# Fused attention and Mish MLP on one core: a planned issue order replaced by a fixed list, with paired last query steps

## Chip, core and metric

One core of one Trainium2 chip. The metric is device time in microseconds (us) of one execution. Engines: PE is TensorE, DVE is VectorE, ACT is ScalarE, POOL is GpSimd, SP is SyncE, which here only issues DMAs.

## What is computed

```python
q_rot, k_rot = rotate(q), rotate(k)          # 4 batches, 8 heads, 576 positions, 64 wide
attn = softmax(q_rot @ k_rot.T / 8)
x = (attn @ v).transpose(0, 2, 1, 3).reshape(2304, 512)
h = x @ w_in                                 # 512 x 2048
g = h * tanh(softplus(h))                    # Mish
out = g @ w_out                              # 2048 x 512
```

## The kernel before

**Work.** Heads go in pairs, P = 0 to 15, four pairs to a batch. A pair's 576 queries are five steps: t = 0 to 3 of 128 queries, t = 4 of 64. A step (`step`, L744; `exact_step`, L725, for batch 0) has PE make the scores of both heads (`scores`, L626), DVE the row maxima (L656), ACT the exponentials with their row sums (L658), and DVE the sum plus 1e-9 and the reciprocal (L667, L669), one head at a time. At t = 4 the two heads of a pair share one score tile: 64 rows each, written by 64x64 matmuls for P < 8 (float32), and by a block-diagonal copy of the queries, `xd`, for P >= 8 (three terms, L642).

From batch 1 on, the weights of the softmax are split into two float16 parts (`weights_hi` on POOL or ACT, `weights_lo` on DVE, L679) in the tile `ew`, and a transposing DMA turns them. At t = 4, DVE first copies the second head's 64 rows to the upper partitions (L766). Batch 0 is turned by PE instead (`turned`, L683), with copies out of PSUM on ACT or DVE. `av` (L772) multiplies by V and leaves x as two float16 parts, for queries 0 to 255 (half 0) and 256 to 575 (half 1).

**The MLP** runs per batch and half, c = 0 to 7. `h_unit` makes 16 first products of 12 matmuls (L1014), ACT the Mish (L1019), `h_split` two float16 parts g (L1029, L1033). `p_sub` makes 16 second products of 12 matmuls (L1050); after every fourth ACT scales the result out (L1058) and issues the store.

**Weights.** Both arrive as 64-bit floats, 2 MB for each of four quarters of `w_in` and of `w_out`. A quarter is staged in a `Home` (tiles that are idle at that time: g, parts of w2, xt, stg, qk), its maximum is taken (L870), and it is decoded in four blocks by `decode` (L900): ACT scales the high words (L908); POOL, ACT or DVE shifts the low words (L910 to L913); DVE merges twice (L914, L917); ACT or DVE makes the first float16 part (L924); POOL or DVE the second (L928). That is 32 blocks in all. A quarter's load waits until the tiles of its home are read out.

**Order.** The program first lists all operations with their dependencies and the engines they may run on (`Plan.op`, L183). Then `Plan.order` (L220) plays a model of the engines, with priorities shifted by the table `ORDER` (L70), and fixes each engine's sequence. While its model has PE idle before 130 us, it puts matmuls on the identity matrix (fills, L1166) ahead of the next PE operation. FRONT, SLOTS and the W1/W2 lists (L31 to L51) set where steps, loads and decoding enter the list.

Of the kernel before, what the change touches and what calls it, by code (L numbers as in the profile page):

```python
# [30 lines left out]
W1L = [0, 0, 0, 2]  # L31
W1S = [3, 5, 3, 4]
W1D = [4, 10, 6, 9]
VA = 4
W2L = [3, 4, 6, 4]
W2D = [9, 13, 10, 13]
PRE0 = 15
WSH = 2
FRONT = 13
TR = 107 / 128  # L40
ALPHA = 7.992
SLOTS = [
    [1, 2, 4, 7, 12, 13, 13, 15, 16, 17, 17, 20, 21, 26, 26, 28, 29, 31],
    [10, 10, 12, 13, 14, 17, 18, 22, 23, 25, 28, 29, 31],
# [8 lines left out]
LATE = 24  # L53
PREP = [7, 5, 0, 13]
PSH = [25, 1, 822]
# [3 lines left out]
WARM = 130000  # L59
SKEEP = 1  # L60
QH = [[0], [0], [0, 1], [1], [0, 1]]
CUT = 320
SWITCH = 1400
DWELL = 920.788
PEN = 800
PENP = 183.99
HOLD = 0
PE, ACT, DVE, POOL, SP = "PE", "ACT", "DVE", "POOL", "SP"
ROPED = (0,)
ORDER = {}  # L70
for _row in """
    load_ident: =-891.8
    load_cs: 0=-4725.3 1=-2736.9
    prep_k: 0=-1685.8 1=1345.9 2=-3283.2 3=-1440.2 4=-2527.3 5=1365.9 6=-3350.9 7=-727.6 8=7228.2 9=1123 10=4507.3
        11=2436.8 12=1246.7 13=1266.3 14=531.9 15=-496
    prep_q: 0=-830.4 1=-2158.7 2=191.3 3=-532.3 4=894.2 5=1315.9 6=3277.5 7=923.3 8=5272.9 9=1626 10=4380.1 11=390.1
        12=5017.8 13=-412.3 14=-701.7 15=568.3
    load_v: 0=3994.1 1=5478 2=4090 3=4703.6 4=1637.8 5=6310.7 6=1937 7=2445.7 8=6111.3 9=6287.7 10=6432.3 11=6598.3
        12=1354.1 13=3922.6 14=5016.1 15=521.1
    w1_load: 0=3231.7 1=2580 2=2629.3 3=2601.7  # L80
    step: 0_0=-5011.8 0_1=-3915.2 1_0=-899.4 1_1=-3704.2 2_0=-768.3 2_1=-4320.3 3_0=-57 3_1=-170.5 0_2=1152
        0_3=-3148.4 0_4=-1518.5 1_2=2864.7 1_3=517.3 1_4=1108.3 2_2=776.3 2_3=-820.2 2_4=-3724.7 3_2=2490.2
        3_3=-1004.1 3_4=2186.6 4_0=-10265.9 4_1=-6834.6 4_2=-9928.1 4_3=-8511 4_4=-8735.2 5_0=-5295.7 5_1=-2535.4
        5_2=909.3 5_3=-4406.8 5_4=-1375 6_0=-4151.1 6_1=-1144.1 6_2=-446.8 6_3=-2426.2 6_4=-479.5 7_0=-5518.7
        7_1=-1224.1 7_2=-2119.2 7_3=-6982.4 7_4=-2612.3 8_0=-3202.1 8_1=-1414 8_2=204.1 8_3=2292.3 8_4=1625.1
        9_0=-5959.7 9_1=-4121.4 9_2=-6528.3 9_3=-2553.3 9_4=-6549.4 10_0=619.3 10_1=4327.5 10_2=-1607.1 10_3=641
        10_4=3369 11_0=1381.8 11_1=4866.8 11_2=1584.4 11_3=4685.9 11_4=4821.5 12_0=183.8 12_1=130.2 12_2=440
        12_3=981.1 12_4=-4305.9 13_0=-2179.5 13_1=-1019.4 13_2=-2104.5 13_3=1203.6 13_4=1964.2 14_0=255.3 14_1=-3296.6
        14_2=-1022.2 14_3=-3430.1 14_4=-4749.2 15_0=7309.3 15_1=12247.6 15_2=9741.9 15_3=12817.5 15_4=7465.4
    w1_scale: 0=-4916.9 2=-4591.2 3=-7163 1=-6494.3  # L90
    w2_load: 0=3752.3 1=6199.2 3=1533.5 2=4425.7
    v_amax: 0=-205.1 1=770.6 2=6910.8 3=384.2
    w1_decode: 0=-373 2=274.9 3=-427.1 1=494.1
    undo_h: 0_0=2142.2 0_2=2646.4 0_3=-6332.5 0_1=-910 1_0=-17085.8 1_1=-10926.9 1_2=-11192.1 1_3=-10149.8
# [24 lines left out]
        1_0_0=7256.9 1_0_1=724.9 1_0_2=2708.6 1_0_3=5613.4 1_1_0=5578.5 1_1_1=-240.8 1_1_2=2524.8 1_1_3=4870.4
        1_2_0=-2595.2 1_2_1=2569.1 1_2_2=1251.7 1_2_3=2314.6 1_3_0=8909.1 1_3_1=2527.9 1_3_2=6624.3 1_3_3=8988.5  # L120
        2_0_0=5216.6 2_0_1=4475.8 2_0_2=6685.1 2_0_3=5076.5 2_1_0=2015.2 2_1_1=3967.5 2_1_2=2759.6 2_1_3=-1754.1
        2_2_0=-543.3 2_2_1=-3395.8 2_2_2=-202.5 2_2_3=-415.9 2_3_0=7117.2 2_3_1=7249.2 2_3_2=10558.9 2_3_3=6213.1
        3_0_0=10859.4 3_0_1=5235.1 3_0_2=12710 3_0_3=10851 3_1_0=3502.5 3_1_1=1964.6 3_1_2=7713.4 3_1_3=2290.2
        3_2_0=5627.6 3_2_1=4044.1 3_2_2=9651 3_2_3=2737.6 3_3_0=7888.6 3_3_1=8394.5 3_3_2=7665.7 3_3_3=5875.7
        4_0_0=-4710 4_0_1=-2995.9 4_0_2=-5881.4 4_0_3=1495 4_1_0=-6282.1 4_1_1=-3702.9 4_1_2=-4565.5 4_1_3=-5568.9
        4_2_0=-6959.7 4_2_1=-2649.4 4_2_2=-7915.8 4_2_3=-6054.9 4_3_0=-3152.9 4_3_1=-4740.5 4_3_2=-4199.3
        4_3_3=-4966.3 5_0_0=14545 5_0_1=14291.9 5_0_2=11395.3 5_0_3=10935.1 5_1_0=6312.3 5_1_1=9174.9 5_1_2=9637.9
        5_1_3=5647.9 5_2_0=12241.2 5_2_1=12166.9 5_2_2=12886 5_2_3=11735.9 5_3_0=7624.5 5_3_1=8020.9 5_3_2=6252.4
        5_3_3=6168.9 6_0_0=-1296.8 6_0_1=3206.9 6_0_2=-632.5 6_0_3=-1529.1 6_1_0=-859.6 6_1_1=-6570.2 6_1_2=213.9
        6_1_3=2618.8 6_2_0=669.3 6_2_1=-3715.1 6_2_2=-1554.2 6_2_3=-4042.8 6_3_0=-3273.1 6_3_1=-2869.2 6_3_2=-2331.1  # L130
        6_3_3=-5740.2 7_0_0=-6397.6 7_0_1=-446.9 7_0_2=-1868 7_0_3=-3467.9 7_1_0=-4286.8 7_1_1=351.8 7_1_2=-3439.6
        7_1_3=-3211.1 7_2_0=4885.5 7_2_1=8695.8 7_2_2=4219.3 7_2_3=4981.7 7_3_0=832.9 7_3_1=5696.5 7_3_2=7682
        7_3_3=7800.5
""".split():
    if _row.endswith(":"):
        _kind = _row[:-1]
    else:
        _key, _at = _row.split("=")
        ORDER[f"{_kind}_{_key}" if _key else _kind] = float(_at)


class Buf:
# [7 lines left out]
    def __call__(self):  # L150
        if self.ap is None:
            self.ap = self.make()
        return self.ap


class Plan:


    LATENCY = {PE: 197, ACT: 152, DVE: 128, POOL: 150, SP: 0}

    def __init__(self):
        self.ops, self.rings, self.shift, self.banks = [], {}, 0, []
        self.blk, self.names, self.base, self.name = 0, {}, {}, ""

    def mark(self, *name):
        self.name = name = "_".join(str(x) for x in name)
        self.blk = self.names.setdefault(name, len(self.names))
# [1063 lines left out]
```

## Time and profile before

| | us |
|---|---|
| median of 3 runs (lowest to highest) | 643.03 (642.48 to 644.96) |
| the profiled execution | 642.61 |
| its span, first to last instruction | 640.8 |
| PE busy in the span | 614.2 |
| ACT, DVE, POOL busy | 449.4, 417.7, 258.4 |

The span is what the profile explains; 1.8 us of the profiled execution lie outside it. Busy time is that in which at least one instruction of an engine runs. Consecutive instructions of an engine overlap a little, so the durations in a group add up to more than the busy time they make. Fills count as busy PE time, though they compute nothing.

### The profile page before, as it was taken

The numbers are of one execution on the slowest core, as the hardware profiler recorded it, in microseconds if no ns is written. First come the engines' busy times: TensorE is split into PE (matmuls) and PEld (weight loads), VectorE is DVE, ScalarE is ACT, GpSimd is POOL, SyncE is SP. The second block draws the span as 40 slices with busy tenths as digits, with TensorE's granted clock in tenths as the row PEclk, the third lists the DMA queues.
The fourth block names the chain that finished last, engine by engine and source line by source line (L and its number), as shares of the span: only waits on it lengthen the run. The fifth ranks groups of instructions, "written<-read, shape, count | busy, mean of one in ns | idle before, by whom it ended". The sixth has DMA issues, their size and how long they took to land. (4 is left out here: it accounts for less than half of the span.)

```text
span 640.8 us, 13358 instructions
## 1 busy us (share of the span) xinstructions
PE 614.2 (96%) x5259; PEld 458.7 (72%) x5259; DVE 417.7 (65%) x958; ACT 449.4 (70%) x851; POOL 258.4 (40%) x251
## 2 busy tenths in 40 slices
PE   4899989999999999999999999999999999999997
PEld 3666656776776666688787776788877767887775
DVE  4999899777668878866676657776377775120310
ACT  2789898989778997588886874878579746421520
POOL 3599869676845243252646144522121210000000
PEclk9989999999999999999999999999999999999999
DMA  8995134344388659674388247643483557000000
GB/s 307 423 402 199 52 104 168 125 143 151 112 177 175 160 102 191 138 153 105 97 164 193 57 118 131 143 93 54 76 126 56 115 114 137 1 19 27 0 11 32
DMA packets 143583, 82.52 MB, mean 129 GB/s; under 512 B 128160, under 2 KB 133920, under 8 KB 141984
## 3 DMA queue, kind: packets, MB, share of 16 engines
q1 hardware_dynamic: 138912, 76.95, 49.0%
q10 hardware_dynamic: 4608, 4.72, 2.4%
q8 instruction: 41, 0.67, 0.4%
q14 instruction: 22, 0.18, 0.1%
HBM read 45.09 MB, written 4.72 MB: 78 GB/s over the span
## 5 line engine op out<-in xcount | busy, mean ns | idle before, releaser
L1050 PE MATMUL bank<-g,w 128*128 128x256 f16 (+1 forms) x1536 | 197.7, 286 | 0.0
L1014 PEld LDWEIGHTS <-w 128*128 128x128 f16 x1536 | 148.2, 98 | 44.3 <-issue 7.6
L1050 PEld LDWEIGHTS <-w 128*128 128x128 f16 x1536 | 146.8, 98 | 44.7 <-issue 8.3
L1014 PE MATMUL bank<-xt,w 128*128 128x256 f16 (+1 forms) x1332 | 171.6, 286 | 0.4 <-ACT mh L1019 0.3
L658 ACT ACTIVATE e<-pair,mx 128x576 f32<-128x576 f32 x144 | 105.5, 737 | 38.5 <-DVE mx L656 33.5
L656 DVE TENSOR_REDUCE mx<-pair 128x1 f32<-128x576 f32 x144 | 103.4, 750 | 30.2 <-PE pair L648 28.2
L673 POOL TENSOR_SCALAR ew<-e,rs 128x576 f16<-128x576 f32 x62 | 47.3, 767 | 185.7 <-DVE rs L669 99.9
L679 DVE SCALAR_TENSOR_TENSOR ew<-e,rs,ew 128x576 f16<-128x576 f32 x108 | 99.1, 941 | 16.0 <-POOL ew L673 9.2
L548 POOL TENSOR_TENSOR raw<-raw,cs 128x576 f32<-128x576 f32 (+2 forms) x60 | 86.4, 1461 | 41.6 <-DMA raw<-in_qk 41.4
L648 PE MATMUL pair<-qk 64*128 64x288 f32 (+1 forms) x704 | 86.4, 365 | 2.3 <-ACT e L658 2.0
L1033 DVE SCALAR_TENSOR_TENSOR g<-mh,cells,g 128x512 f16<-128x512 f32 (+1 forms) x64 | 54.2, 857 | 48.7 <-ACT g L1029 48.3
L1019 ACT ACTIVATE mh<-bank,cells 128x320 f32<-128x320 f32 (+1 forms) x111 | 52.3, 499 | 35.4 <-PE bank L1014 34.1
L648 PEld LDWEIGHTS pair<-qk 64*128 64x128 f32 (+1 forms) x704 | 55.1, 182 | 24.7 <-issue 11.8
L667 DVE TENSOR_SCALAR sm<-sm 128x1 f32<-128x1 f32 x144 | 21.2, 150 | 46.6 <-ACT e L658 46.1
L1058 ACT ACTIVATE ot<-bank,cells 128x256 f32<-128x256 f32 (+1 forms) x32 | 15.9, 495 | 42.7 <-PE bank L1050 40.8
L675 ACT ACTIVATE ew<-e,rs 128x576 f16<-128x576 f32 x46 | 35.0, 771 | 13.2 <-ACT e L658 5.6
L1029 ACT ACTIVATE g<-mh,cells 128x640 f16<-128x640 f32 (+1 forms) x53 | 41.1, 777 | 2.5 <-PE bank L1050 1.5
L1166 PEld LDWEIGHTS <-ident 128*128 128x128 f16 x287 | 27.8, 101 | 17.3 <-DMA ident<-in_ident 8.2
L793 PE MATMUL bank<-et,v 128*64 128x256 f16 (+1 forms) x288 | 39.8, 288 | 0.0
L794 PE MATMUL bank<-et,v 128*64 128x256 f16 (+1 forms) x288 | 39.8, 288 | 0.0
L658 ACT ACT_TABLE_LOAD x28 | 35.9, 1283 | 3.8 <-DVE mx L656 3.3
L1019 ACT ACT_TABLE_LOAD x29 | 37.2, 1283 | 0.5
(128 smaller groups left out, 769.9 us busy)
## 6 DMA issues: line engine op xcount, KB each, us to landing
raw<-in_qk SPq DMA_DIRECT2D x30, 576.0 KB, 4.3
w<-in_w_in SPq DMA_DIRECT2D x4, 1024.0 KB, 11.5
stg<-in_v SPq DMA_DIRECT2D x12, 320.0 KB, 3.3
stg<-in_vflat SPq DMA_DIRECT2D x9, 384.0 KB, 3.0
w<-in_w_out SPq DMA_DIRECT2D x3, 1024.0 KB, 5.9
out_dram<-ot ACTq DMA_DIRECT2D x16, 160.0 KB, 1.8
g<-in_w_in SPq DMA_DIRECT2D x2, 1024.0 KB, 15.6
xt<-in_w_out SPq DMA_DIRECT2D x2, 1024.0 KB, 5.7
```

The lines of the kernel that those rows point to most:

```text
L548: e.tensor_tensor(out=t()[:, :, s], in0=t()[:, :, s], in1=cs()[:, :, s], op=ALU.mult)
L648: nc.tensor.matmul(out, x[own, q], y[own, s], **kw)
L656: op((DVE, dve_ns(S), lambda: nc.vector.tensor_reduce(m(), pt()[:, :, :HS], axis=AX.XY, op=ALU.max, negate=True)), w=[m], r=[pt])
L658: op((ACT, act_ns(S, psum=True, ptr=2), lambda: nc.scalar.activation(e().rearrange("p (c s) -> p c s", c=2), pt()[:, :, :HS], AF.Exp, bias ...
L673: op([(POOL, 1.27 * S, lambda: nc.gpsimd.tensor_scalar(w()[:, c], e(), r()[:, h:h + 1], 1.0, op0=ALU.mult, op1=ALU.mult), 1), (ACT, act_ns ...
L679: op((DVE, dve_ns(S) + 180, lambda: nc.vector.scalar_tensor_tensor(out=w()[:, c], in0=e(), scalar=r()[:, h:h + 1], in1=w()[:, hc], op0=ALU ...
L793: nc.tensor.matmul(po()[0:64, :n], V()[:, vi, c, 0:64], et[:, c, :], start=False, stop=last)
L1014: nc.tensor.matmul(hp(), w1()[:, wi, cc, f:f + 128], x()[:, xi, cc, q0:q0 + n], start=cc == 0 and a == 0, stop=cc == NCC - 1 and a == 2)
L1019: op((ACT, act_ns(n, psum=True, ptr=1), lambda j=j, hp=hp: nc.scalar.activation(hn()[:, j, :n], hp(), AF.Mish, scale=uh())), w=[(hn, j)], ...
L1029: op([(ACT, act_ns(2 * n, ptr=1), lambda: nc.scalar.activation(g()[:, 0, f, :n], hn()[:, :, :n], AF.Copy, scale=f32(gs))), (DVE, dve2_ns(2 ...
L1033: op((DVE, dve_ns(2 * n) + 61, lambda: nc.vector.scalar_tensor_tensor(out=g()[:, 1, f, :n], in0=hn()[:, :, :n], scalar=f32(gs), in1=g()[:, ...
L1050: nc.tensor.matmul(pp()[:, :n], w2e[e]()[:, wi, f], g()[:, gi, f % 8, :n], start=f == 0 and a == 0, stop=f == NF - 1 and a == 2)
```

## The change

1. The planner goes. The issue order is a list of 2296 entries: operation number, the engine among its choices, the PSUM tile, the fills ahead of it.

```diff
-FRONT = 13
+FRONT = 12
...
+ORDER = """
+    59 58 3 5 2 11 6 4 92 137b 108 20 107 119 32 109 131c 12 7 110@0 19 8b 111 112 113 114@1+3 13 115 116 14 118@2 9
+    15 159 136@3 10b 125b 120 64@45+10 25 23 124@0 138 45 121 63 21 65 62 67 66 156 16b 68 139 130@1 78@45+5 69 24 126
...
+        for row in ORDER.split():
+            n, way, slots, fill = re.fullmatch(r"(\d+)([a-c]?)(?:@(\d+))?(?:\+(\d+))?", row).groups()
+            o = self.ops[int(n)]
+            for b, i in zip(o["takes"], slots or ""):
+                b.slots = (int(i),)
+            if fill:
+                self.fill(o["takes"][0], int(fill))
+            o["ways"]["abc".index(way or "a")][2]()
```

With the operations numbered in the order in which the changed program lists them, the new list reads as follows. It has 77 fills, the last at entry 280. The first MLP product is entry 387. The first second product is entry 492, the last of half 0 entry 845; half 1's first products begin at entry 851. Entries count from 0.

2. Steps with t = 4 are made for two pairs at once: 64 rows of each pair, one score tile per head. Eighteen steps to a batch instead of twenty.

```diff
+        heads = [P] if t < 4 else [P, P + 1]
+                            to = slice(0, 128) if whole else slice(64 * i, 64 * i + 64)
+                            nc.tensor.matmul(pts[h]()[to, c, :HS], x[own, q], y[own, s], **kw)
-            for a in range(2):
-                c = 2 * a * S
-                op((DVE, 215, lambda c=c: nc.vector.tensor_copy(ew()[0:64, c + S:c + 2 * S], ew()[64:128, c:c + S]), 1),
-                   w=[(ew, 2 + a)], r=[(ew, a)])
-seq += [(P, t) for P in range(NP, NPAIR) for t in range(5)]
+seq += [(P, t) for P in range(NP, NPAIR) for t in range(5) if t < 4 or P % 2 == 0]
```

For P >= 8 the block-diagonal matmuls of 128 rows become matmuls of 64 rows per head, twice as many. Each pair keeps its own transposing DMA of 64 rows.

3. Sum and reciprocal take both heads in one instruction each (`inverse`).

```diff
-        for h in range(n):
-            c = slice(h, h + 1)
-            op((DVE, 125, lambda c=c: nc.vector.tensor_scalar(sm()[:, c], sm()[:, c], 1e-9, scale, op0=ALU.add, op1=ALU.mult)),
+        op((DVE, 125, lambda: nc.vector.tensor_scalar(sm()[:, 0:n], sm()[:, 0:n], 1e-9, scale, op0=ALU.add, op1=ALU.mult)),
```

4. In the numbering, `mlp` lists the first products of both halves of batch 0, then both second products. The g of half 0 lives in `xt[1]` and in `stg` instead of the g tiles.

```diff
+        if c == 0:
+            yield from mlp_h(0)
+            yield from mlp_h(1)
+        elif c == 1:
+            yield from mlp_p(0)
+            yield from mlp_p(1)
```

5. Homes of the weights: quarter 3 of `w_in` goes to the g tiles after quarter 0; quarter 1 of `w_out` to the tiles of its quarter 0; quarter 2 to one of them and two qk tiles; quarter 3 to two qk and two raw tiles. Batch 1's V is staged in the raw tiles.

```diff
-            3: lambda: Home(xt_home(), stg_home(), stg_home())}[fq]()
+            3: lambda: Home(g_home(0), g_home(1))}[fq]()
-            1: lambda: Home(xt_home(st["w1", 3].tiles()[:1]), stg_home(), stg_home()),
+            1: lambda: Home(*[w2_home(k, [st["w2", 0].tiles()[k - 2]]) for k in (2, 3)]),
-            3: lambda: Home(xt_home(st["w2", 1].tiles()[:1]), stg_home(), stg_home())}[e]()
+            3: lambda: Home(qk_home(), qk_home(), raw_home(), raw_home())}[e]()
```

6. DVE becomes a choice for more operations: the first part of the softmax weights, scaling and first part of V, x, the result of the second product.

```diff
+            (DVE, dve2_ns(S, ptr=1), lambda: nc.vector.tensor_scalar(w()[:, c], e(), r()[:, h:h + 1], None, op0=ALU.mult), 1)],
+            (DVE, dve2_ns(640), lambda: nc.vector.tensor_copy(o()[:, 0], tv()), 1)], w=[(o, 0)], r=[t])
```

In the list DVE takes 30 of 108 such softmax parts, 26 of 64 first parts of g, 19 of 32 results, 13 of 32 x, and 11 of 32 first parts of the weights (all 11 after entry 387).

## Rows read from the trace of the kernel before

**Rows 1.** The page: busy time per engine, share of the span, instructions.
```profile
PE 614.2 (96%) x5259; PEld 458.7 (72%) x5259; DVE 417.7 (65%) x958; ACT 449.4 (70%) x851; POOL 258.4 (40%) x251
```

**Rows 2.** Windows by stage: us, busy per engine (instructions), clock, DMA share, GB/s.
```profile
0.00:114.77 114.77, 96.05 (x749) 66.77 (x749) 98.28 (x267) 88.74 (x191) 85.60 (x87) 0.99 0.63 235
114.77:142.00 27.23, 26.53 (x235) 20.44 (x235) 21.73 (x65) 26.05 (x51) 19.63 (x16) 1.00 0.42 139
142.00:200.00 58.00, 58.00 (x486) 41.69 (x484) 40.06 (x106) 45.68 (x88) 39.37 (x36) 1.00 0.58 146
200.00:340.00 140.00, 139.00 (x1232) 102.81 (x1229) 105.82 (x232) 112.44 (x206) 52.66 (x52) 1.00 0.70 144
340.00:540.00 200.00, 197.20 (x1767) 149.91 (x1765) 136.46 (x268) 145.23 (x264) 61.17 (x63) 1.00 0.55 106
540.00:640.80 100.80, 97.46 (x803) 77.10 (x800) 15.39 (x23) 31.21 (x56) 0.00 (x0) 1.00 0.06 18
```

**Rows 3.** PE timeline near the first MLP product: start, us, instructions (neighbours left out).
```profile
106.69 1.19 PE L648 MATMUL pair<-qk 64*64 64x288 f32 x8
107.80 0.44 PE L704 MATMUL bank<-ident,e 128*64 128x128 f32 x4
...
114.77 8.02 PE L1014 MATMUL bank<-xt,w 128*128 128x256 f16 x72
122.72 1.24 PE L648 MATMUL pair<-qk 64*128 64x288 f32 x8
123.89 2.79 PE L1014 MATMUL bank<-xt,w 128*128 128x256 f16 x24
```

**Rows 4.** Groups by shape, 0 to 114.77 us: count, busy us, mean ns, idle before.
```profile
L1166 PE MATMUL bank<-ident 128*128 128x256 f16 x201 | 25.1, 273 | 1.1 <-DVE ew L716 0.6 <-DVE w L917 0.5
L656 DVE TENSOR_REDUCE mx<-pair 128x1 f32<-128x576 f32 x28 | 20.2, 749 | 3.5 <-PE pair L648 3.4
L658 ACT ACTIVATE e<-pair,mx 128x576 f32<-128x576 f32 x26 | 19.1, 739 | 5.9 <-DVE mx L656 5.8
L1166 PE MATMUL pair<-ident 128*128 128x256 f16 x86 | 13.6, 311 | 8.4 <-DMA ident<-in_ident 8.2 <-ACT et L698 0.2
L924 ACT ACTIVATE w<-w 128x512 f16<-128x512 f32 x14 | 9.3, 670 | 5.0 <-DVE w L917 4.9
L928 POOL TENSOR_TENSOR w<-w,w 128x512 f16<-128x512 f32 x8 | 9.2, 1169 | 3.0 <-ACT w L924 3.0
L870 DVE TENSOR_REDUCE cells<-w 128x1 f32<-128x1024 f32 x7 | 8.5, 1208 | 0.0
L908 ACT ACTIVATE bank<-w,cells 128x512 f32<-128x512 f32 x12 | 8.5, 729 | 0.6 <-DVE cells L497 0.6
L914 DVE SCALAR_TENSOR_TENSOR bank<-bank,w 128x512 uint32<-128x512 uint32 x12 | 8.0, 688 | 0.3 <-ACT bank L908 0.3
L917 DVE SCALAR_TENSOR_TENSOR w<-w,bank 128x512 int32<-128x512 int32 x12 | 8.0, 676 | 0.5 <-DVE bank L914 0.5
L870 DVE TENSOR_REDUCE cells<-stg 128x1 f32<-128x512 f32 x6 | 4.0, 676 | 0.0
L667 DVE TENSOR_SCALAR sm<-sm 128x1 f32<-128x1 f32 x26 | 3.7, 145 | 1.2 <-ACT e L658 1.2
```

**Rows 5.** DVE timeline: two maxima in a row.
```profile
13.71 1.42 DVE L656 TENSOR_REDUCE mx<-pair 128x1 f32<-128x576 f32 x2 [2.11 <-PE pair L648]
```

**Rows 6.** DVE line L1030, all of it: durations ns min/median/max.
```profile
L1030 DVE TENSOR_SCALAR g<-mh,cells x11: 478/486/956, 123.5 to 598.1; 128x512 f16<-128x512 f32 x7, 128x640 f16<-128x640 f32 x4
```

**Rows 7.** Windows of 2 us where the granted clock falls, columns as in Rows 2.
```profile
30.00:32.00 2.00, 0.81 (x5) 0.50 (x5) 2.00 (x7) 1.81 (x4) 2.00 (x3) 1.00 0.99 419
...
34.00:36.00 2.00, 1.77 (x8) 1.18 (x8) 1.83 (x4) 1.53 (x4) 2.00 (x3) 0.50 1.01 405
```

**Rows 8.** The page: DMA issues of weights, KB each, median us from issue to landing.
```profile
w<-in_w_out SPq DMA_DIRECT2D x3, 1024.0 KB, 5.9
...
g<-in_w_in SPq DMA_DIRECT2D x2, 1024.0 KB, 15.6
```

More of the change, by code (lines that the diff above doesn't have):

```diff
@@ L142 @@
+"""
 class Buf:
@@ L156 @@
 class Plan:
-    LATENCY = {PE: 197, ACT: 152, DVE: 128, POOL: 150, SP: 0}
     def __init__(self):
[L162 to L167, printed above, removed]
+        self.ops, self.rings, self.banks = [], {}, []
     def tile(self, pool, shape, dt, tag, bufs=1):
@@ L218, in op, with issue @@
         return o["n"]
-    def order(self):
-        ops = self.ops
-        for o in ops:
+    def issue(self):
+        for o in self.ops:
             for b in set(o["bufs"]):
@@ L246, in order @@
-        ready_at = [0.0] * len(ops)
-        free = dict.fromkeys((PE, ACT, DVE, POOL, SP), 700.0)
-        ring_free = dma_free = 0.0
-        lanes = [0.0] * 8
-        window, busy, warm = 0, 0.0, False
-        port = dict.fromkeys((DVE, POOL), 0.0)
-        blocked = dict.fromkeys(free, 0.0)
-        pending = [(0.0, o["n"]) for o in ops if not wait[o["n"]]]
-        heapq.heapify(pending)
-        ready, issued, now = {e: [] for e in free}, [], 0.0
-        done = [False] * len(ops)
-        table, since, last = "exp", 0.0, 0.0
@@ L487, in tiny @@
     def tiny(out, r, fn):
-        op((DVE, 70, fn), w=[out], r=r)
+        op((DVE, 110, fn), w=[out], r=r)
         return out
@@ L515, in max_exponent @@
         got = small() if out is None else Buf(lambda: out[0]()[:, out[1]:out[1] + 1], of=out[0])
-        op((DVE, 70, lambda: nc.vector.tensor_copy(got(), pb()[:, 0:1])), w=[out or got], r=[pb])
+        op((DVE, 140, lambda: nc.vector.tensor_copy(got(), pb()[:, 0:1])), w=[out or got], r=[pb])
         got.part = out and out[1]
@@ L681, in weights_lo, with turned @@
            w=[(w, part)], r=[e, (r, h), (w, hpart)])
-    def turned(es, rows, n, et, at, key, r, R):
+    def turned(es, to, r):
+        full = slice(0, 128)
         for h in range(2):
@@ new lines, in places @@
+    def places(P, t):
+        k = 0 if t < 2 else 1
+        new = [P] if t in (0, 2) and (P, k) not in done else [P + 1] if t == 4 else []
+        for p in new:
+            done.add((p, k))
+            et_tile(p, k, *((F32, 9) if P < NP else (F16, 18)))
+            if P < NP:
+                ew = sbuf((128, 4 * S), F16, "ew", EW)
+                st["R", p, k] = Buf(lambda ew=ew: ew().bitcast(F32), of=ew)
+        at = 128 * t - AVH[k][0]
+        if t < 4:
+            return [(P, k, at, slice(0, 128))]
+        return [(P, k, at, slice(0, 64)), (P + 1, k, at, slice(64, 128))]
@@ new lines, in attention_mish_mlp, with step @@
+    done = set()
+    def step(P, t):
+        exact = P < NP
+        to = places(P, t)
+        ew = None if exact else sbuf((128, 4 * S), F16, "ew", EW)
+        sm = sbuf((128, 2), F32, "sm", 3)
+        es = [max_exp(pt, h, sm) for h, pt in enumerate(scores(P, t))]
+        r = inverse(sm, 2, 1.0 if exact else 2.0 ** -15)
+        if exact:
+            turned(es, [(st["ET", p, k], at, t, st["R", p, k], q) for p, k, at, q in to], r)
+            return
+        for h in range(2):
+            weights_hi(ew, h, slice(h * S, h * S + S), es[h], r, h)
+        for h in range(2):
+            weights_lo(ew, 2 + h, h, slice((2 + h) * S, (3 + h) * S), slice(h * S, h * S + S), es[h], r, h)
+        for p, k, at, q in to:
+            n = q.stop - q.start
+            et = st["ET", p, k]
+            op((SP, turn_ns(n * 4 * S * 2), lambda et=et, at=at, q=q, n=n: nc.sync.dma_start_transpose(
+                out=et()[:, :, at:at + n], in_=ew()[q])), w=[(et, t)], r=[(ew, j) for j in range(4)])
@@ L998, in h_unit @@
         uh = sc["uh", b, u // 2]
-        if u == 0:
-            ml["g", c] = [g_tile(k) for k in range(2)]
+        if u % 2 == 0:
+            g_part(c, u // 2)
         hn = sbuf((128, 2, 320), F32, "mh", 3)
@@ L1057, in p_sub @@
             uo = sc["uo", b, e]
[L1058 removed]
+            op([(ACT, act_ns(n, psum=True, ptr=1), lambda: nc.scalar.activation(o()[:, :n], pp()[:, :n], AF.Copy, scale=uo())),
+                (DVE, dve_ns(n) + 61, lambda: nc.vector.tensor_scalar(o()[:, :n], pp()[:, :n], uo(), None, op0=ALU.mult))],
                w=[o], r=[pp, uo])
```

650 lines of the change are left out of this document (238 added, 412 removed).

## The prediction

> **What bounds the kernel now.** I read the page's busy shares first [rows 1]: PE is busy for 614.2 of 640.8 us, so at first sight nothing but PE's own work can shorten the run. But fills count as busy. The groups of the first stage [rows 4] show 201 + 86 = 287 of them, 25.1 + 13.6 = 38.7 us, all in that stage. Useful PE work is therefore 614.2 - 38.7 = 575.5 us, and 65.3 us of the span are lost: idle or fills.
>
> The windows by stage [rows 2] show where. The first ends at 114.77 us, where the first MLP product starts [rows 3]. There PE is busy for 96.05 us, 38.7 of them fills: useful 57.3, lost 57.4. From there to 142 us the loss is 0.7, and from 142 to the end 0 + 1.0 + 2.8 + 3.3 = 7.1 us. So after 142 us the kernel is bound by PE work and a new order can win at most some 4 us there (3.3 us of the 7.1 are the last window, with the evacuation and the store of the end). Before 114.77 us it is bound by the vector engines: DVE is busy for 98.3 us of 114.8, ACT 88.7, POOL 85.6 [rows 2]. They do not only what the first product needs. By the groups of line L914 in that stage 28 of all 32 decoding blocks are merged there, the 12 of the row and 16 on other tiles, though a first product needs only the 16 of `w_in`; and 28 row maxima (L656) have been taken [rows 4].
>
> **The change, part by part.**
>
> *The list, first product at entry 387.* I counted the list's entries ahead of it: 10 steps instead of 15 (18 maxima against 28), 17 blocks merged instead of 28, 8 sums and 8 reciprocals for two heads each instead of 26 and 26, 11 reductions of weights (1.208 each) instead of 12 long and 8 short ones (0.676). DVE: 11 x (0.688 + 0.676) = 15.0; 10 x 0.749 = 7.5; 36 x 0.145 = 5.2; 12 x 1.208 + 8 x 0.676 - 11 x 1.208 = 6.6 [rows 4]. Of 267 instructions 143 are left; the other 47 that go (copies from PSUM, rope, small scales) cost between 0.145 and the stage's mean of 98.28 / 267 = 0.37, so 7 to 17; I take 11. Sum 45.3 us of durations. Neighbours overlap: two maxima of 0.749 take 1.42 [rows 5], 0.08 less each, 10 us for 124 instructions. DVE keeps 98.3 - 35 = 63 us. At the 86% at which it worked in this stage that is 73 us.
>
> ACT: 11 scalings at 0.729, 15 first parts at 0.670, 8 exponentials at 0.739 [rows 4], 33 others at the mean of 88.74 / 191 = 0.46, together 39 us, less 6 for overlap: 56 us are left, at its 77% again 72 us. POOL: 17 second parts at 1.169 and 16 others at 0.98: 50 us left, 67 us. The three agree, so I take **73 us for the first product** (68 if DVE works at 92%, 80 if at 79%). PE's useful work ahead of it: 10 scores at 1.17 (start to start [rows 3]), four `av`, the transposes and sums of 8 steps: about 40 us. Lost: 73 - 40 = 33 instead of 57.4 us.
>
> *From the first product to entry 851*, where half 1 begins, PE has 32 MLP products of 1.32 ((8.02 - 2.79) / 4 per 12 matmuls [rows 3]), 42 us, 11 scores, 13 us, and 29 us of turning and `av`: 84 us. DVE has 15 blocks, 24 maxima, 12 splits, the second parts of x and the rest of `w_out`'s maxima: 91 us in durations of the same rows, 76 with the overlap. So PE leads by little. Bounds of the loss: 0.7 us as in the second window; 11 us if DVE works at 80% as it does there (76 / 0.80 = 95). I take 6, between them, since second products now wait for blocks that are decoded just before.
>
> *Paired last steps.* For P < 8, eight steps of 1.1 us (106.69 to 107.80 [rows 3]) become four. Each holds eight matmuls of 64x64 that use all four corners of the array, where two at a time ran before. Nothing won if corners of the same rows take turns, 4 x 1.11 = 4.5 us if all four run at once; a loss is excluded, since the matmuls are the same. I take 4.5: the scores of t < 4 run two row halves at once on twice the columns in 1.17 us. The Trainium skill, TensorEngine Tiling (Array Packing), "Tile-to-Partition Mapping", counts 64x64 as four independent tiles; no row here has all four at work. For P >= 8 twice the matmuls on half the rows: no change. The 24 copies that DVE loses, the halved sums and the same transposing DMAs lie where DVE is busy for 68 to 76% and PE for 98 to 100% [rows 2]: nothing.
>
> *More choices for DVE.* After entry 851 nothing, by the same cover; without it each moved copy would be worth its 0.5 us. Ahead of it eleven first parts of weights go from ACT (0.670) to DVE. Line L1030 shows the copy of that kind: median 0.486, one of 0.956 [rows 6]. I charge 0.07 each, 0.8 us in all, inside the 6.
>
> *Order of the two halves.* The numbering puts half 1's first products ahead of half 0's second ones, but the list does not: 492 to 845 come before 851. So I price this at nothing but the homes that it moves.
>
> *Queues.* SP issues `w_in`'s quarter 0 first, ahead of the rope tables; quarter 3 waits for the g tiles of quarter 0. No wait of that kind shows in the rows; between 0 and a landing of 15.6 us [rows 8], I take 0, as its first use stands 42 entries further on.
>
> **Sum.** 575.5 - 4.5 = 571.0 useful; lost 33 + 6 + 7.1; 617 us of span. The profiled execution adds 1.8: **619 us**, against 642.6 for the one profiled and 643.0 for the median. Some 0.5%, 3 us, is what a measurement can tell from no change.
>
> **Rivals.**
>
> *The clock.* With 77 fills for 287, PE may fall to its lower level in the front. At 30 to 32 us PE was busy for 0.81 of 2 us, and at 34 to 36 us the granted clock was 0.50, 1.2 GHz [rows 7]. If half of the 40 us of useful front work runs there, PE needs 20 us more; half of that lies in the chains of scores, maxima and transposes that the vector engines wait on: 619 + 10 = 629. Against it: real PE work is 40 of 73 us. Chance 0.17.
>
> *DVE and POOL in each other's way.* If all eleven DVE copies in the second stage wait for a POOL instruction of 1.169 us [rows 4], DVE has 13 us more: 89, and the loss there is 14 instead of 6: 627. The Trainium skill, SBUF — State Buffer, "Who interferes with whom", says that the loser of the port shared by DVE and GpSimd blocks fully. Median and minimum of L1030 (0.486, 0.478) speak against that as the usual case, its 0.956 for it. Chance 0.06.
>
> *The front is only stretched.* Vector work decides until `w_out` is decoded. If DVE then works at 69%, as from 142 to 200 us, its 76 us take 110, and PE idles between products: loss 26, 639 us; 643 without the 4.5 of the corners. Chance 0.09.
>
> *Slower: loads behind decoding.* Four quarters wait for tiles that decoding must first read out (`w_in` 3, `w_out` 1 to 3), and DVE's reductions of them stand in a fixed queue, so that all behind them waits. Fully exposed, by the landings [rows 8], 15.6 + 3 x 5.9 = 33 us: 652. It decides from 24 us of exposure, three quarters of it. The list leaves 26 entries between the reissue for quarter 1 of `w_out` and its first reduction, some 4 us of DVE: too little to hide a landing of 5.9, enough to hide most of it. Chance 0.11.
>
> **How the numbers follow.** Forecast 0.57, and the four rivals. Faster by over 0.5% (below 640): forecast, clock, port: 0.80. The front only stretched ends at the edge: same, 0.09. Slower 0.11. The range reaches down to 606 (first product at 68 us, loss of 1 in the second stage, 5 in the rest) and up to 638: the clock's 629 with 9 of the forecast's upper bounds (4.5 of the corners, 5 of the second stage). That leaves the last two cases out.
>
> **What would show it.** Right: the first L1014-type product near 73 us; fills of some 8 to 10 us; half 1's first products near 163 us with PE lost time of about 39 us by then; DVE near full from 15 to 150 us; eight 64x64 matmuls in some 1.2 us. The clock rival shows in windows with a granted clock near 0.5 after 40 us; the loads as DVE idle behind a DMA of `in_w_in` or `in_w_out`. The prediction is wrong if the first product stands beyond 85 us, or if PE loses more than 20 us between it and entry 851.

## The result and the profile after

The changed kernel takes 625.62 us (median; 624.54 to 626.89), the kernel before 643.91 us on the same chip: a ratio of 0.9718, 95% interval 0.9689 to 0.9748. The forecast said 619 us and faster. The sign, the main step and the range hold; the figure is 6.6 us too low, and a run that undoes one term of it takes 5.9 us less. The profiled execution has a span of 623.9 us. Each run below stands with its ratio to the kernel before, measured on the same chip as that run.

The page's busy times of the changed kernel, to be read beside [rows 1]:

```profile
PE 592.5 (95%) x5065; PEld 440.5 (71%) x5065; DVE 460.6 (74%) x897; ACT 400.5 (64%) x774; POOL 236.4 (38%) x214
```

The odd figure is DVE's: 61 instructions fewer than before, but 43 us more of busy time. Most of it is the work that part 6 of the change gave it (420.7 us in a run below that takes this back); 11 us are waits inside DVE's instructions (449.6 us in a run without them). The windows by stage, columns as in [rows 2], cut at the first MLP product (77.49 us) and at half 1's first one (168.45 us):

```profile
0.00:77.49 77.49, 58.20 (x387) 37.70 (x387) 66.31 (x143) 56.27 (x124) 51.67 (x54) 0.98 0.72 274
77.49:168.45 90.96, 86.59 (x723) 63.57 (x722) 87.33 (x209) 68.29 (x138) 55.47 (x50) 1.00 0.31 103
168.45:200.00 31.55, 29.89 (x245) 19.93 (x244) 28.57 (x52) 27.11 (x49) 13.49 (x13) 1.00 0.90 207
200.00:340.00 140.00, 137.69 (x1224) 103.24 (x1223) 121.93 (x222) 101.64 (x193) 64.72 (x57) 1.00 0.74 155
340.00:520.00 180.00, 179.68 (x1666) 136.63 (x1665) 134.06 (x238) 117.72 (x219) 51.09 (x41) 1.00 0.58 116
520.00:623.90 103.90, 100.50 (x835) 79.41 (x829) 22.45 (x37) 29.49 (x55) 0.00 (x0) 1.00 0.12 27
```

By these time marks forecast and trace compare stretch by stretch: 73 us forecast to the first product, 77.5 measured; 90 (84 + 6) to half 1's first product, 91.0 measured; 454 from there to the end (617 - 163), 455.5 measured. What stood at 114.77 us before [rows 3] stands 37 us earlier, the end only 17 us. Of the 37 us, 12.5 are useful PE work that merely moved behind the mark: 57.3 us stood ahead of it before, 58.20 less 13.4 of fills, or 44.8, now. The loss ahead of it fell by 24.7 us, from 57.4 to 32.7. Behind it some is given back: PE loses 4.4 us up to half 1's first product, where DVE is busy for 87.33 of 90.96, against 0.7 in the second window of [rows 2], and its useful work counts 3.6 us more than before.

Further views show where the 4.5 us of the first stretch went. First single lines with all their instructions: durations (min/median/max, ns), first and last start, form. They are the sum of one head in the kernel before; then, in the changed kernel, the sum of two heads, its reciprocal, and the second part of x, with one of two inputs in PSUM (`bank`) and with both in SBUF (`ew`, `xt`):

```profile
L667 DVE TENSOR_SCALAR sm<-sm x144: 129/153/157, 16.2 to 538.1; 128x1 f32<-128x1 f32 x144
...
L517 DVE TENSOR_SCALAR sm<-sm x72: 149/169/1385, 19.1 to 523.4; 128x2 f32<-128x2 f32 x72
...
L519 DVE RECIPROCAL rs<-sm x72: 139/156/167, 19.8 to 524.8; 128x2 f32<-128x2 f32 x72
...
L665 DVE SCALAR_TENSOR_TENSOR xt<-bank,xt x24: 404/448/484, 182.8 to 550.2; 128x256 f16<-128x256 f32 x12, 128x320 f16<-128x320 f32 x12
L665 DVE SCALAR_TENSOR_TENSOR xt<-ew,cells,xt x8: 475/544/1697, 65.0 to 166.9; 128x256 f16<-128x256 f32 x4, 128x320 f16<-128x320 f32 x4
```

The sums again as a group of the changed kernel (count | busy, mean ns | idle before):

```profile
L517 DVE TENSOR_SCALAR sm<-sm 128x2 f32<-128x2 f32 x72 | 29.5, 410 | 20.1 <-ACT e L509 20.1
```

One sum of two heads (128x2) takes 410 ns in the mean, half of them 169 or less, the longest 1385; one of 128x1 took 145 [rows 4] and never over 157. The reciprocal on the same two columns has a median of 156 and a maximum of 167. What a long one waits for is read from the timelines of DVE and POOL side by side (start, us):

```profile
102.02 0.47 DVE L517 TENSOR_SCALAR sm<-sm 128x2 f32<-128x2 f32 x1
...
104.79 0.73 DVE L517 TENSOR_SCALAR sm<-sm 128x2 f32<-128x2 f32 x1
105.44 0.15 DVE L519 RECIPROCAL rs<-sm 128x2 f32<-128x2 f32 x1
...
106.21 1.08 DVE L755 TENSOR_SCALAR qk<-qk 128x512 int32<-128x512 int32 x1
```

```profile
101.08 1.38 POOL L771 TENSOR_TENSOR w<-g,w 128x512 f16<-128x512 f32 x1 [3.25 <-ACT w L767]
...
104.35 1.15 POOL L771 TENSOR_TENSOR w<-g,w 128x512 f16<-128x512 f32 x1
105.46 1.54 POOL L383 TENSOR_TENSOR raw<-raw,cs 128x640 f32<-128x640 f32 x1
```

102.02 + 0.47 is 102.49, and POOL's instruction ends at 102.46; 104.79 + 0.73 = 105.52 against 105.50; the shift, 106.21 + 1.08 = 107.29 against 107.00. Each began while POOL's was running; the two sums ended 0.02 to 0.03 us after it, the shift of 512 columns 0.29. The whole trace says the same of the sums: 26 of the 72 take over 0.2 us, and every one of them began while a POOL instruction ran and ended 0.02 to 0.03 us after that ended. In the kernel before 73 of the 144 sums of 128x1 also began while POOL was running, and none took over 0.157 us.

### The profile page after: what moved, and what is told of

It is laid out like the page before. It is cut to its first block, busy times and chain, and to the rows that moved or that the text cites. A ratio compares the mean times of both kernels' runs of the same rounds, so it can differ in the third digit from the quotient of the medians.

```text
span 623.9 us, 12751 instructions
## 1 busy us (share of the span) xinstructions
PE 592.5 (95%) x5065; PEld 440.5 (71%) x5065; DVE 460.6 (74%) x897; ACT 400.5 (64%) x774; POOL 236.4 (38%) x214
## 5 line engine op out<-in xcount | busy, mean ns | idle before, releaser
L873 PE MATMUL bank<-xt,w 128*128 128x320 f16 (+1 forms) x1392 | 181.1, 286 | 0.2 <-DVE xt L665 0.2
L909 PE MATMUL bank<-g,w 128*128 128x320 f16 (+1 forms) x1344 | 176.5, 288 | 0.0
L383 POOL TENSOR_TENSOR raw<-raw,cs 128x576 f32<-128x576 f32 (+2 forms) x61 | 90.7, 1499 | 44.3 <-DMA raw<-in_qk 37.2
L892 DVE SCALAR_TENSOR_TENSOR g<-mh,cells,g 128x640 f16<-128x640 f32 (+1 forms) x56 | 51.1, 926 | 52.6 <-ACT g L888 52.4
L878 ACT ACTIVATE mh<-bank,cells 128x256 f32<-128x256 f32 (+1 forms) x116 | 55.2, 499 | 44.8 <-PE bank L873 38.5
L523 POOL TENSOR_SCALAR ew<-e,rs 128x576 f16<-128x576 f32 x29 | 24.7, 855 | 130.2 <-DVE rs L519 70.1
L517 DVE TENSOR_SCALAR sm<-sm 128x2 f32<-128x2 f32 x72 | 29.5, 410 | 20.1 <-ACT e L509 20.1
L638 PEld LDWEIGHTS <-v 128*64 128x64 f16 x288 | 29.6, 110 | 8.4 <-issue 5.7
L387 POOL TENSOR_TENSOR raw<-raw 128x288 f32<-128x288 f32 x32 | 31.1, 980 | 0.9
L918 DVE TENSOR_SCALAR ot<-bank,cells 128x320 f32<-128x320 f32 (+1 forms) x19 | 9.8, 515 | 28.0 <-PE bank L909 19.5
```

Source lines behind the costliest of these rows:

```text
L383: e.tensor_tensor(out=t()[:, :, s], in0=t()[:, :, s], in1=cs()[:, :, s], op=ALU.mult)
L638: nc.tensor.matmul(po()[0:64, :n], V()[:, vi, c, 0:64], et[:, c, :], start=False, stop=last)
L873: nc.tensor.matmul(hp(), w1()[:, wi, cc, f:f + 128], x()[:, xi, cc, q0:q0 + n], start=cc == 0 and a == 0, stop=cc == NCC - 1 and a == 2)
L878: op((ACT, act_ns(n, psum=True, ptr=1) + 40, lambda j=j, hp=hp: nc.scalar.activation(hn()[:, j, :n], hp(), AF.Mish, scale=uh())), w=[(hn, ...
L892: op((DVE, dve_ns(2 * n) + 61, lambda: nc.vector.scalar_tensor_tensor(out=gv()[:, 1, f, :n], in0=hn()[:, :, :n], scalar=f32(gs), in1=gv()[ ...
L909: nc.tensor.matmul(pp()[:, :n], w2e[e]()[:, wi, f], gv()[:, gi, f % 4, :n], start=f == 0 and a == 0, stop=f == NF - 1 and a == 2)
```

## The experiments

**Products beside decoding: the main step.** The same list, with the 72 operations of half 0's MLP moved behind the last decoded block and the PSUM banks dealt out anew.

```diff
-    444 357@3 360 333 445 386 409@45 358 446 300 387 533@1 402@2 ...
+    ... 788@45 739b 835 728b 778 740 533@3 514@0 801 534 620@2 ...
```

> The changed kernel's list with the 72 operations of half 0's MLP (both products, mish, splits, outputs) held back until the last block of w_out is decoded, nothing else removed; PSUM banks dealt out anew. If the gain comes from products that run beside the decoding (the forecast's main step): PE has some 89 us of useful work left ahead of the last decoded block, which comes at about 153 us (165 less the 12 us that DVE gave to half 0), so it loses about 64 us there instead of 37; first MLP product near 150 us, time 643 to 655 us, no better than before. If the gain comes from there being less vector work (paired last steps, sums and copies of two heads at once), wherever the products stand: 622 to 632 us.

666.06 us, ratio 1.0361 (1.0308 to 1.0414): slower than the kernel before. First MLP product at 159.43 us. The window that ends there, and the one behind it (columns as above):

```profile
77.49:159.43 81.94, 55.98 (x338) 33.31 (x338) 75.67 (x190) 46.80 (x105) 51.56 (x48) 0.83 0.31 99
159.43:662.60 503.17, 491.43 (x4344) 376.88 (x4342) 319.13 (x565) 294.83 (x544) 131.48 (x113) 1.00 0.51 106
```

PE is busy for 55.98 of 81.94 us where it had 86.59 of 90.96, and the granted clock falls to 0.83. The work is the same, only its place and the PSUM banks differ, so products beside decoding are what the change lives on. The 40 us are not the step's worth, since nothing else in the list was rearranged to fit. It went 11 us beyond the expected range: the clock in the front is one cause, 12 us of idle time behind 159 us another; how they divide is open.

**The sum of two heads.** First split into two instructions of one column, at the same place of the list:

```diff
-        op((DVE, 125, lambda: nc.vector.tensor_scalar(sm()[:, 0:n], sm()[:, 0:n], 1e-9, scale, op0=ALU.add, op1=ALU.mult)),
+        op((DVE, 250, lambda: [nc.vector.tensor_scalar(
+            sm()[:, h:h + 1], sm()[:, h:h + 1], 1e-9, scale, op0=ALU.add, op1=ALU.mult) for h in range(n)]),
```

> The changed kernel with the sum of two heads (one 128x2 instruction, mean 410 ns, minimum 149, maximum 1385) split into two of 128x1. If the 128x2 form waits for a running POOL instruction and the 128x1 form does not: each takes about 150 ns, two together 0.25 to 0.30, DVE is busy 6 to 10 us less over the run, of which some 30 steps lie ahead of half 1's first product; the first product comes 1 to 3 us earlier and the time is 622 to 625 us. If the long ones are a wait for the row sums that ACT has yet to write: the first of each two stays near 410, DVE is busy 10 us more, and the time is the same or 1 to 2 us longer.

619.75 us, ratio 0.9620 (0.9595 to 0.9645): 5.9 us less than the changed kernel with one instruction more per step. All 144 sums of this kernel, and its windows at its own time marks:

```profile
L517 DVE TENSOR_SCALAR sm<-sm x144: 130/143/155, 19.3 to 516.3; 128x1 f32<-128x1 f32 x144
```

```profile
0.00:71.98 71.98, 54.53 (x386) 35.48 (x387) 63.70 (x151) 55.88 (x124) 51.91 (x54) 1.00 0.79 295
71.98:161.53 89.55, 85.26 (x722) 63.04 (x722) 85.20 (x220) 68.24 (x138) 55.58 (x50) 1.00 0.32 105
161.53:616.90 455.37, 448.36 (x3960) 339.30 (x3957) 300.70 (x600) 275.91 (x513) 129.80 (x111) 1.00 0.55 114
```

No sum waits any more. The first product comes 5.5 us earlier, half 1's 6.9, and the last stretch is as long as it was (455.4 against 455.5). Both sums stand behind the same two exponentials as the one did, so it was not a wait for ACT's row sums. The time is below the range of the expectation (622 to 625).

Is it the width or the form? The same 128x2 sum with two inputs in SBUF (the 1e-9 left out where the scale is not 1):

```diff
+        op((DVE, 125, lambda: nc.vector.scalar_tensor_tensor(
+            out=sm()[:, 0:n], in0=sm()[:, 0:n], scalar=1e-9 if scale == 1.0 else scale, in1=sm()[:, 0:n],
+            op0=ALU.add if scale == 1.0 else ALU.mult, op1=ALU.max if scale == 1.0 else ALU.min)),
```

> The changed kernel with the 128x2 sum as one scalar_tensor_tensor (same tile as both inputs; the 1e-9 is left out where the scale is not 1) instead of a tensor_scalar. If only the tensor_scalar form waits for a running POOL instruction: each near 150 ns like the 128x2 reciprocal, DVE busy some 18 us less than in the changed kernel, 617 to 620 us. If any form with its data in SBUF and more than one element per row waits, as the rows of the weights' second parts suggest (797 ns at least, 1971 at most): mean near 400 again and 624 to 627 us.

625.60 us, ratio 0.9715 (0.9684 to 0.9745), and the sums as before:

```profile
L517 DVE SCALAR_TENSOR_TENSOR sm<-sm 128x2 f32<-128x2 f32 x72 | 27.4, 380 | 20.0 <-ACT e L509 19.9
```

So two forms of a 128x2 sum wait for POOL; the 128x2 reciprocal (139 to 167 ns) and the sums of 128x1 do not. The two groups of L665 shown above fit: with one input in PSUM no instruction takes over 484 ns, though eight of the 24 began while POOL was running; with both in SBUF one takes 1697. The Trainium skill, SBUF — State Buffer, "Who interferes with whom", says that a DVE instruction in a mode that uses both of its ports, or with two SBUF inputs beside a GpSimd instruction that reads SBUF, needs a port pair that it shares with GpSimd, and that the later one blocks fully; VectorE: DVE Perf Modes, "Mode 2×_2P — use both read ports for one tensor", lets a `tensor_scalar` into that mode when its data lie in SBUF and the outermost dimension of more than one element is even, or odd and equal in source and destination. Two columns are even, and the runs agree with both pages; that a row of one element does not wait is what the runs show.

The clock is a rival for those 6 us: in the changed kernel PE waits 1.36 us at 66.64 us for the reciprocal behind such a sum, and then runs at half clock. Windows of 2 us there:

```profile
66.00:68.00 2.00, 1.15 (x13) 0.70 (x13) 2.00 (x10) 1.09 (x4) 1.79 (x4) 1.00 0.20 81
68.00:70.00 2.00, 2.00 (x12) 1.66 (x12) 1.81 (x6) 1.75 (x7) 2.00 (x2) 0.67 0.02 4
70.00:72.00 2.00, 2.00 (x10) 1.42 (x10) 1.34 (x5) 1.72 (x3) 0.62 (x1) 0.50 0.03 8
```

Twelve fills more ahead of the product that waited:

```diff
-    372 327@4 456 292 308@1 345@0 373 329 262 457 328 310 458@2 346 343@5 347 374 459 332 293 325@0 391 344 311 375@2
+    372 327@4+12 456 292 308@1 345@0 373 329 262 457 328 310 458@2 346 343@5 347 374 459 332 293 325@0 391 344 311 375@2
```

> The changed kernel with 12 more fills at the sum product ahead of which PE waited 1.36 us for DVE, at 66.6 us; behind that wait the granted clock was .67 and .50 for 4 us. If the 6 us that the split sums gave back were in good part the clock: no window under .95 between 60 and 80 us, first MLP product 1.5 to 2.5 us earlier, 622 to 624 us. If they were DVE's waits on POOL, with the clock only following: the clock may stay up, but the first product moves by under 1 us and the time is 624.5 to 627 us.

The clock stays at 1.00 from 60 to 80 us (it falls at 18 to 24 us instead) and the first product comes 2.25 us earlier (75.24), but the time is 626.33 us, ratio 0.9693 (0.9655 to 0.9732): no gain that can be told from none. Between half 1's first product and the end this execution takes 459.1 us instead of 455.5; one place in it is a wait of 2.19 us for a transposing DMA at 225 us that took 1.02 in the changed kernel. The run with two inputs separates the two as well: its sums wait, but no window of 2 us from 10 to 100 us in its trace has a clock below 1.00.

```profile
0.00:75.11 75.11, 54.15 (x386) 35.30 (x387) 67.37 (x143) 56.74 (x124) 51.65 (x54) 1.00 0.74 283
```

Its first product comes at 75.11 us, too, and its time is that of the changed kernel (625.60). Of the 5.5 us at the first product, then, some 2.3 are the clock that follows DVE's wait, the rest the waits; at the end only the split sums paid.

**The corners.** Two other orders of issue for a paired last step.

```diff
+                    turns = [(i, h) for i in range(len(each)) for h in range(2)]
+                    if not whole:
+                        turns = [(0, 0), (1, 1), (0, 1), (1, 0)]
```

> The changed kernel with the four corners of a paired last step (64x64 each) issued diagonal by diagonal instead of pair by pair of row halves. The paired step took 1.97 us from start to start, against 1.11 for each single one before. If all four corners can run at once and only the order of issue kept them apart: about 1.1 us for a paired step, 3 to 4 us less over four of them in stages where DVE, not PE, decides, so 622 to 625 us. If never more than two corners run at once: 1.9 to 2.0 us again and the same time within 0.3%. If the old order already overlapped something that the new one loses: up to 3.9 us for a step, and 626 to 632 us.

626.40 us, ratio 0.9712 (0.9688 to 0.9735): no difference. And with the split sums, all of one pair ahead of the other:

```diff
-                for c in range(2):
+                if not whole:
+                    turns = [(c, i) for i in range(len(each)) for c in range(2)]
+                for c, i in turns:
```

> The kernel with two 128x1 sums, and the 64x64 matmuls of a paired last step issued head pair by head pair, so that the first eight run on one half of the columns and the next eight on the other. If four corners run at once only when four different ones stand next to each other: 1.9 to 2.1 us for a paired step instead of 1.20, 3 us more PE work over four steps. If that counts in full, as the forecast has it (4.5 us off PE's useful work): 622 to 623.5 us. If DVE sets the end of these stages and hides it: 619 to 621 us, with the longer steps in the trace. If the steps still take 1.20 us: nothing is said, 619.75 us.

619.36 us, ratio 0.9583 (0.9552 to 0.9614), against 619.75: the edit did nothing. The paired steps in the PE timelines of the changed kernel, the diagonal order and this one:

```profile
84.58 2.04 PE L499 MATMUL pair<-qk 64*64 64x288 f32 x16
129.43 1.20 PE L499 MATMUL pair<-qk 64*64 64x288 f32 x16
```

```profile
84.38 1.86 PE L502 MATMUL pair<-qk 64*64 64x288 f32 x16
129.05 1.20 PE L502 MATMUL pair<-qk 64*64 64x288 f32 x16
```

```profile
80.46 1.22 PE L502 MATMUL pair<-qk 64*64 64x288 f32 x16
124.49 1.22 PE L502 MATMUL pair<-qk 64*64 64x288 f32 x16
```

The first of these two expectations rested on a misreading: the 1.97 us of the changed kernel's first paired step is not its work. The instruction at L760 still reads that PSUM pair until 85.37 us (84.70 + 0.67), and PE stands for 0.7 us in the middle of the step, which the timeline counts as busy. An undisturbed paired step takes 1.20 us in any order, 1.13 from start to start (168.52 to 169.65 in the kernel with split sums). In all three orders the sixteen records start in four groups of four, each group within 0.04 us and some 0.25 us after the last, where the kernel before shows groups of two. So four corners do run at once, and what it would cost if they did not can't be had by reordering.

**The fills.** Both kernels without them.

```diff
-        for _ in range(m):
+        for _ in range(0):
```

> The changed kernel without its 77 fills (13.4 us busy), all else the same. If the fills stand only in waits and the clock does not need them: 625.6 us within 1%, first MLP product at 77 us, some 6 to 9 fewer us of PE busy time than 13.4 since part of it overlaps neighbours. If they hold the clock up (the rival 'clock' of the forecast): the granted clock of the first 77 us falls from .98 to about .7, the 45 us of useful products there take up to 20 us more, and the time is 630 to 640 us. One figure between: the trace of the changed kernel already has a stretch at .50 around 70 us, which should become longer.

630.08 us, ratio 0.9777 (0.9749 to 0.9805), 4.5 us more.

> The kernel before without its 287 fills (38.7 us busy), order and slots unchanged. If the front is bound by DVE, ACT and POOL, as the forecast says: first MLP product near 115 us still, 643 us within 0.5%, and the lost time of the front is idle instead of fills. If the fills carry the clock: granted clock of the first 115 us near .6, useful work of 57 us stretched by up to 20 to 30 us of which half shows: 650 to 660 us.

658.52 us, ratio 1.0233 (1.0199 to 1.0268), 14 us more; in the profiled execution, which at 663.38 us is the longest of the four, the first product moves from 114.77 to 129.87 us. The windows of its front:

```profile
0.00:40.00 40.00, 14.49 (x65) 8.91 (x65) 25.78 (x63) 20.04 (x38) 19.25 (x26) 0.81 0.95 374
40.00:80.00 40.00, 31.74 (x149) 18.13 (x151) 33.66 (x91) 32.59 (x71) 33.34 (x32) 0.67 0.53 180
80.00:129.87 49.87, 39.58 (x250) 23.27 (x246) 40.97 (x116) 36.86 (x84) 33.69 (x32) 0.81 0.30 111
```

At a granted clock between .67 and .81 the scores and transposes come late, and DVE works at 77% of its time instead of 86% [rows 2]. So the front before was bound by chains through PE as well as by DVE. In the changed kernel the front loses only 1.2 us without fills (first product at 78.74), at a clock of .93. Why so little isn't shown; real work that fills PE sooner is likely. The other 3 us or more are lost behind 169 us, and what ties them to the fills is open.

**The added choices for VectorE.** All 73 uses back on ScalarE; one row of the list that changes:

```diff
-    469@1 530@4 470 471 689b 857@3 472 532 813 529 57 591 507@1 531b 690 858 476c 810@5 487@0 508b 747 493@3 489 693
+    469@1 530@4 470 471 689 857@3 472 532 813 529 57 591 507@1 531b 690 858 476c 810@5 487@0 508b 747 493@3 489 693
```

> The changed kernel with the 73 uses of the choices for VectorE that the change added (30 first parts of the softmax weights, 19 outputs, 13 first parts of x, 11 of v) set back to ScalarE; 69 of them stand behind half 1's first product, where PE is 98 to 100% busy. If they are worth nothing there: the time of the changed kernel within 0.5% (623 to 629 us), ACT busy some 45 us more, DVE some 35 less. If ACT then holds up the exponentials or mish: PE idles in the stages after 168 us, 630 to 640 us. If DVE's relief from waits on POOL counts for more than ACT's load: 619 to 622 us.

635.66 us, ratio 0.9861 (0.9826 to 0.9896): 10 us more. The front is unchanged (half 1's first product at 167.25 us); behind it the profiled execution, at 638.04 us the longest of six, takes 469 us instead of 455.5. PE's longest waits there:

```profile
PE pair L499 <- ACT e L509: 4.2, 5, 1.6
PE pair L499 <- ACT mh L878: 1.7, 1, 1.7
PE bank L909 <- DVE g L892: 1.4, 1, 1.4
```

In the changed kernel the first of them is 0.5 us. ACT has 38 us more to do, reads the score tiles late, and the next scores wait for their PSUM. Only half of the loss shows as idle time of PE: behind half 1's first product its idle time grows from 7.7 to 14.1 us and its busy time from 447.8 to 454.9 for as many instructions. A wait inside a step counts as busy, as in the paired step above; that this is all of the 7 us isn't shown.

**Taking more from DVE.** On top of the split sums, first the sums of batch 0's 18 steps left out, whose scale is 1 and whose 1e-9 is added to at least 1:

```diff
-            sm()[:, h:h + 1], sm()[:, h:h + 1], 1e-9, scale, op0=ALU.add, op1=ALU.mult) for h in range(n)]),
+            sm()[:, h:h + 1], sm()[:, h:h + 1], 1e-9, scale, op0=ALU.add, op1=ALU.mult) for h in range(n) if scale != 1.0]),
```

> The kernel with two 128x1 sums (619.75 us), and the instruction left out altogether in the 18 steps of batch 0, where the scale is 1 and 1e-9 is added to a sum that is at least 1. If DVE's work sets the end of the first two stages: 36 instructions of 0.144 us less, some 3 to 5 us of DVE time there, first product 1 to 2 us and half 1's first product 2 to 4 us earlier, 616 to 618 us. If PE or the chains through ACT set it: 619 to 621 us.

616.89 us, ratio 0.9572 (0.9537 to 0.9607). Then DVE's six shifts of decoding given to ACT, the first of them:

```diff
-    59 58 3 5 2 11 6 4 92 137b 108 20 107 119 32 109 131c 12 7 110@0 19 8b 111 112 113 114@1+3 13 115 116 14 118@2 9
+    59 58 3 5 2 11 6 4 92 137b 108 20 107 119 32 109 131b 12 7 110@0 19 8b 111 112 113 114@1+3 13 115 116 14 118@2 9
```

> The same as the run before, and the six DVE shifts of decoding (128x512 int32: 0.42 us alone, up to 1.76 where a POOL instruction runs; 5.9 us in all) given to ScalarE at 0.69 us each. If waits on POOL in DVE's two-input-free forms still set the pace: 1 to 4 us less than the run before (613 to 617 us). If ACT, busy for 68 of 90 us there, delays the exponentials by as much: the same within 0.3%, or 1 to 3 us more.

614.63 us, ratio 0.9542 (0.9506 to 0.9577), the best of all, though the two intervals overlap. Last, half 0's four first parts of g that stand on DVE given to ACT as well, the first of them:

```diff
-    390@0 264 425@45 400 568 392 593 650 651@3 393 604 686 426 401 361@1 428 652 667@2 683b 427 424 394b 684 804@0
+    390@0 264 425@45 400 568 392 593 650 651@3 393 604 686 426 401 361@1 428 652 667@2 683 427 424 394b 684 804@0
```

> The kernel without exact sums and with the six shifts on ScalarE (614.63 us), and half 0's four first parts of g that stand on DVE (0.48 us alone, up to 1.76 beside POOL; 4 us in all) on ScalarE at 0.72 each. If waits on POOL still set the pace of the second stage: 612 to 614 us. If ACT, which also has mish and the exponentials, is now as full as DVE: 614 to 617 us.

618.91 us, ratio 0.9614 (0.9581 to 0.9646): 4 us lost again. The second stage in these three, in this order:

```profile
70.99:159.40 88.41, 85.32 (x722) 63.02 (x722) 83.12 (x201) 68.12 (x138) 55.73 (x50) 1.00 0.33 106
```

```profile
72.15:158.07 85.92, 85.17 (x722) 63.04 (x722) 78.41 (x196) 70.62 (x143) 54.66 (x50) 1.00 0.34 109
```

```profile
72.53:161.33 88.80, 86.13 (x722) 63.76 (x722) 77.44 (x192) 72.78 (x147) 54.87 (x50) 1.00 0.32 105
```

With DVE at 78.41 us PE has no slack left there (85.17 of 85.92). The last run has less on DVE and is longer: a second part on DVE now waits 1.8 us for a first part on ACT, and PE waits 1.3 us for such a first part and 0.5 for such a second part, waits that it did not have in the run before. PE's busy time grows by the other 1.0 us of the 2.9, which was not traced. So less work on the leading engine is no gain if its next instruction then waits for another.

## Why the prediction was right, and where it missed

**The main step held.** DVE, ACT and POOL keep 63, 56 and 50 us ahead of the first product, the forecast said; 66.31, 56.27 and 51.67 are measured, and DVE 63.70 once its sums don't wait. With the products held back the whole gain is gone (666.06 us). (A slip on the way: (8.02 - 2.79) / 4 is 1.31, not 1.32; the 42 us stay.)

**The step that failed** is the pricing of the sums: "8 sums and 8 reciprocals for two heads each" entered at the 0.145 us of the 128x1 row [rows 4], and behind entry 851 the halved sums were put at nothing. The 20 sums ahead of half 1's first product take 10.2 us instead of the 2.9 so charged, because a sum of 128x2 waits for a running POOL instruction and one of 128x1 does not. With 128x1 sums the kernel takes 619.75 us, first product at 71.98 us and half 1's at 161.53, where the forecast had 619, 73 and 163.

**The port rival** (627 us, chance .06) had the right mechanism at the wrong instruction. It looked at eleven DVE copies of decoding, and all but one, 0.2 us longer than the rest, don't wait:

```profile
L768 DVE CAST w<-w x6: 411/416/427, 80.7 to 139.1; 128x512 f16<-128x512 f32 x6
L768 DVE CAST w<-g x2: 415/522/628, 91.8 to 99.1; 128x512 f16<-128x512 f32 x2
L768 DVE CAST w<-qk x2: 417/417/417, 143.4 to 159.3; 128x512 f16<-128x512 f32 x2
...
L768 DVE CAST w<-raw x1: 415/415/415, 163.6 to 163.6; 128x512 f16<-128x512 f32 x1
```

POOL itself waits for these copies (10.0 us in six waits), so it often isn't running then. The sums, which nothing on POOL waits for directly, meet whatever POOL does. The charge of 0.8 us belonged to them, and was 7. That 627 is nearer to the result than 619 is luck: it rests on a loss of 14 us between the first product and entry 851, where 4.4 were lost.

**Between the first product and entry 851** the forecast's length was good (90 against 90.96), its reason not: "PE leads by little", with 76 us for DVE. DVE has 87.33 (85.20 with split sums) and leads, as the runs show that take work from it. Added up, its instructions take 102.3 us there, where the forecast had 91, and 13.3 us of this is what they take beyond the shortest of their line and shape. The sums have 3.6 us of that, five shifts of decoding 2.5, four first parts of g 2.4, the second parts of x the next most. So the length came out right in good part by luck.

**Paired last steps** were priced right: eight at 1.11 against four at 1.13 is 4.4 us less, 4.5 in the forecast. How much of it reaches the end, two of the four being in a stage where DVE leads, wasn't settled. TensorEngine Tiling (Array Packing) of the Trainium skill, cited in the prediction, counts four independent 64x64 tiles; here they show as 1.20 us for twice the matmuls that took 1.19 [rows 3].

**More choices for DVE: "After entry 851 nothing"** was wrong as a reading; that the last stretch came out right is luck. DVE's share and PE's 98 to 100% do not say that ACT has room; without the choices this list loses 10 us. The sum hid it: the old loss of 7.1 us was carried over, and the choices are part of what keeps it there (7.7 now).

**Useful work of PE** (busy less fills) is 592.5 - 13.4 = 579.1, 576.1 with split sums, where the forecast had 571; the losses ahead of the first product are smaller by as much with the split sums (29.6 instead of 33). That the two errors cancel in the 619 is luck. Subtracting the fills' busy time may take off their overlap with neighbours too, so that both numbers move against each other; this wasn't tested, and the time marks are not touched by it.

**The other rivals.** The clock falls for 4 us only (68 to 72 us), and holding it up gains nothing at the end. The front was not only stretched: DVE works at 96% between the marks, not 69. Loads behind decoding don't show: DVE is idle for 3.6 us in all in that stage.

## What to carry to other kernels

Price an instruction by a row of its own shape. Making one instruction of two is no gain when the wider one waits for another engine and the narrow one does not; look at the maximum beside the median, and lay the other engine's timeline next to the long ones. Where DVE is busy for 96% of a stretch and PE for 95%, busy shares don't say which leads: a run that takes work from one of them does. A busy PE can hide waits, so compare time marks, or instructions per window, before taking busy time for work.

## What was not expected of the hardware

A DVE instruction of two elements per partition took up to 1.385 us, 0.149 at least, since it waited for a POOL instruction; a sum of one element never took over 0.157 us. Four 64x64 float32 corners run at once in any of three orders of issue: 16 matmul records in 1.20 to 1.22 us. And fills that look like waste carried 14 us in the kernel before, by a granted clock of .96 to 1.00 instead of .67 to .81 in its front.
